# Chunk 0's joins: transposed blocks from VectorE, masks on GpSimd, loads and one MLP piece placed anew

## The chip, the cores and the metric

One core of a Trainium2 chip. The metric is the device time in microseconds (us) of one execution; lower is better. "PE" is TensorE (its weight loads are listed as "PEld"), "DVE" VectorE, "ACT" ScalarE, "POOL" GpSimd and "SP" SyncE, which issues most DMAs.

## The reference, cut to what matters

The input is `q`, `k`, `v` (4 batches, 8 heads, 768 tokens, 48 wide), `beta` (4, 8, 768), and two weights, 384x2048 and 2048x384. Everything is float32.

```
k_n = k / (norm(k) + 1e-6)
for t in range(768):                     # for each batch and head
    y[t]  = q[t] @ state
    v_old = k_n[t] @ state
    state = state + beta[t] * outer(k_n[t], v[t] - v_old)
x = y, heads side by side: 3072 tokens x 384
h = x @ w_in                             # 384 -> 2048
out = (h * sigmoid(h)) @ w_out           # 2048 -> 384
```

## The kernel before, in words

The 768 tokens are cut into 6 chunks of 128 tokens, each with two halves of 64 (`hf` is 0 or 1 in the code); the four batches form two groups of two (`g` is 0 or 1). Inside a chunk the recurrence becomes the solution of a triangular system for each batch and head. Its inverse `xi` is made once for a chunk out of blocks of 32 tokens; `inner` (L866) multiplies it with the values to give `z`, `update` (L886) brings the state forward, `old` (L932) and `new` (L945) give the outputs from the old state and from `z`. The outputs are turned into `xT`, the MLP's input with tokens along the free dimension. The MLP is cut into small pieces; one piece of its first half is three products `phid<-xT,w_in` (L1088), half of a bank, and after two pieces ACT applies silu (`gT`, L1098). Each float32 product is recorded as two matmuls and two weight loads.

**The joins of chunk 0.** Chunk 0 does not wait for a state, so its inverse is made by blocks in `joins(hf)` (L1539), a list of stages that are run one after the other. `corner` (L743) multiplies the off-diagonal 16-blocks and DVE adds the correction (L750). `turned` (L759) forms the transposed inverses of 32-blocks, as products, and copies them out of PSUM into `xes[0]` (in the trace `xe_y`), one copy by ACT and one by DVE for each group. `straight` (L772) forms the inverses themselves and copies four tiles for each group into `xi`, half by ACT (L554), half by DVE (L557). `merge_half` (L832) puts 32-blocks together to blocks of 64: the first product uses `xes[0]` and goes to `y`, the second uses `y` and goes to `xi`; each is again copied by one ACT and one DVE copy. PSUM banks come from three rooms: A (names `pl`, `py`, `px`), CC (`pb_c`) and M (`phid`, `pt`).

**After half 0's joins** come `inner` for half 0, then `first_outputs` (L910), whose products `py` become `xT` by an ACT copy (L554) and a DVE addition (L919). They need query blocks `ap`, which have been masked with `above` (L1524): four DVE multiplications of 128x512. Between stand turns of queries (`pt`, L510) that ACT copies to `stage` (L520).

**After that** a text of letters sets the order by hand, in `script`. The letters that matter: `j` is one step of `joins(1)`, `r` one MLP piece (three products), `s` a step of the solution for chunk 0, `f` a step of a narrowing, `b` its beginning, `l` a step of chunk 1's key lengths, `p` a step of its scores (L539), `q` a turn of its queries.

**Weights.** A weight arrives as 768 KB DMAs issued by SP (L292, L304). It is then narrowed: two ACT activations (L233, L234), then DVE operations (L238, L242) and a GpSimd integer addition (L246). A piece `w_in` number i must be narrowed before its MLP piece runs. ACT's two are placed by `begin_next`/`b`, the DVE ones by `fill`/`f`. The loads are in a list: each has a number, and is issued on SP once so many PE instructions have begun (`begun[0]`, 4 for a product, 2 for a turn). SP takes them in order, with the query loads (L144) among them. `pin` keeps each engine's instructions in the order in which the code writes them.

**Scattering.** For half 1 the odd heads' outputs go over `part` (L554), and SP's five DMAs (L925) into `xT`.

Of the kernel before, what the change touches and what calls it, by code (L numbers as in the profile page):

```python
# [19 lines left out]
def kernel(  # L20
# [10 lines left out]
    nc = tc.nc  # L31
# [660 lines left out]
    def invert_first(step):  # L692
# [62 lines left out]
        def turned(g, hf):  # L755

            pls = [bank(room, "pl") for room in (A, CC)]
            for i, n, k in heads(g, hf):
                pin(nc.tensor.matmul(  # L759
                    pls[k][rows[2 * k], T * i : T * (i + 1)], lhsT=up[rows[2 * k], n, :],  # L760
                    rhs=y[rows[2 * k], n, :], start=True, stop=True,
                ))
                yield
            for k, by in enumerate((by_act, by_dve)):
                by(of_half(xes[0][rows[2 * k]], g, hf, k), out_of(pls[k], rows[2 * k], T))

        def straight(g, hf):

            pls = [bank(room, "pl") for room in (A, CC)]
            for i, n, k in heads(g, hf):  # L770
                for j in (2 * k + 1, 2 * k):
                    pin(nc.tensor.matmul(  # L772
                        pls[k][rows[j], T * i : T * (i + 1)], lhsT=y[rows[j], n, :],
                        rhs=up[rows[j], n, :], start=True, stop=True,
                    ))
                    yield
            for odd in (1, 0):
                for k, by in enumerate((by_act, by_dve)):
                    j = 2 * k + odd
                    by(  # L780
# [4 lines left out]
        yield corner, turned, straight  # L785
# [33 lines left out]
    def merge_half(g, hf, second):  # L819
# [15 lines left out]
        for k, by in enumerate((by_act, by_dve)):  # L835
# [666 lines left out]
    for b in range(2, B):  # L1502
# [9 lines left out]
        (WINDOW + PACKET * 8 + -15, fetch_w_in, 6),  # L1512
        (WINDOW + PACKET * 9 + -45, fetch_w_in, 7),
        (WINDOW + PACKET * 10 + -15, fetch_w_out, 2),
        (WINDOW + PACKET * 15 + 45, fetch_w_out, 3),
        (WINDOW + PACKET * 15 + 60, fetch_w_out, 4),
# [5 lines left out]
    def masks(g, u):  # L1522
        to = aps[0, g][1][:, u]
        pin(nc.vector.tensor_tensor(  # L1524
# [3 lines left out]
    for n in range(Q):  # L1528
# [5 lines left out]
        if n == 14:  # L1534
            busy(1, done, Sync)
    corner, turned, straight = next(inv)
# [20 lines left out]
    def none():  # L1557
# [3 lines left out]
        lambda: (size_half(0, pins[seen_on]), begin_next(),),  # L1561
        lambda: (),
        lambda: (),
        lambda: (fill(1), fill(1),),
        lambda: (fill(1),),
        lambda: (),
        lambda: (fill(1),),
        lambda: (fill(1), begin_next(),),
        lambda: (),
        lambda: (),  # L1570
    ]))
    masks(0, 0)
    masks(0, 1)
    masks(1, 0)
    masks(1, 1)

# [150 lines left out]
    for text in (  # L1727
        "s f3 s q q s j32 b j20 r f j8 q f j4 f j16 r j44 b j4 q j4 r f r j22 f j12 f j8 f b j8 f j4 r j20 e r f j99 h f r f2 l s l r l p r l f p l s l2 f r3 l3 p l s l4 p l2 s r l f l4 f l f l2 p l s l2 s f r f r l r l2 p g i p l p f i p f l i r2 i r v f i3 r3 i r i r i3 b r2 f2 r2 i r2 i2 r2 i f b i r i3 f2 r2 f r3 f i2 r f i f r3 f r f i f i2 r i r i k i2 b z r2 i r i r z r i r2 b r t s r b r f s r2 t s m r m t2 r b m f t m s f b r m2 b m f s r m r s m4 s m3 c m4 s r t G m r2 m4 V m s r m r m t2",
# [68 lines left out]
```

## Time and profile before

| what | us |
|---|---|
| median of 3 runs | 631.42 (631.0 to 632.15) |
| the profiled execution's own time | 633.96 |
| its span (first to last instruction) | 631.8 |
| PE busy | 617.7 |
| DVE busy | 415.5 |
| ACT busy | 226.7 |
| POOL busy | 94.0 |

The granted clock of PE was 0.989 on average. Times in the profile count from the start of the span. A row of groups has: line, engine, operation, output and inputs with shapes and count; then busy us and mean ns; then the engine's idle time before them, with what ended it. A row of a timeline or chain begins with the start and the length in us. A row of the windows view has the stretch, its length, then busy us and count of PE, PEld, DVE, ACT and POOL (of PE and PEld alone where one line was asked for), the granted clock as a share of full speed, the share of the DMA engines' time that was busy, and GB/s. A row of the DMA queues has the queue, its kind, packets, MB and share of 16 engines. A row of DMA issues ends with KB each and the us from issue to landing.

### The profile page before, as it was taken

Reading aid. Unit: us, or ns where it says so; the run is one execution under the profiler, and the core shown is the slowest. Engines: PE = TensorE matmul, PEld = TensorE weight load, DVE = VectorE, ACT = ScalarE, POOL = GpSimd, SP = SyncE. Lnnn points to the kernel's source line nnn. Section 1 sums busy time; section 2 is a strip of 40 time slices with the busy share of each in tenths; the row PEclk is TensorE's granted clock in tenths of the full one; section 3 lists DMA queues with packets and bytes.
Section 4 is the critical chain, followed back from the end, with each engine's and each line's share of the span. In section 5 each row is a group of like instructions: output and inputs, shape, how many; then the busy total and the mean of one; then the engine's idle time right before and its main releaser. Section 6 shows DMA issues by size and latency. Waiting matters only on the chain.

```text
span 631.8 us, 21374 instructions
## 1 busy us (share of the span) xinstructions
PE 617.7 (98%) x9390; PEld 543.3 (86%) x9390; DVE 415.5 (66%) x927; ACT 226.7 (36%) x516; POOL 94.0 (15%) x101
## 2 busy tenths in 40 slices
PE   8889989999999999999999999999999999999997
PEld 5578778666799989989989989989989989988997
DVE  6886779999667974546975554976444983345432
ACT  4657873332441122451122451122452122454210
POOL 5234631335020020020020010020002000000000
PEclk9869999999999999999999999999999999999999
DMA  9656506350459360459141359433254024010011
GB/s 175 134 141 199 170 16 149 116 86 4 101 100 186 62 108 4 95 107 188 34 92 20 72 125 156 65 75 44 52 113 95 2 75 62 17 38 1 0 26 26
DMA packets 136941, 52.61 MB, mean 83 GB/s; under 512 B 108672, under 2 KB 130432, under 8 KB 136848
## 3 DMA queue, kind: packets, MB, share of 16 engines
q1 hardware_dynamic: 136512, 51.09, 39.6%
q8 instruction: 74, 1.21, 0.9%
q10 hardware_dynamic: 336, 0.15, 0.1%
q14 instruction: 19, 0.16, 0.1%
HBM read 39.09 MB, written 9.96 MB: 78 GB/s over the span
## 4 chain that ended last, share of the span: by engine, by line
PE 93%; SPq 2%; DMA 1%; issue 1%; ACT 1%; DVE 0%
PE phid L1088 34%; PE px L1200 17%; PE py L1200 13%; PE po L1132 5%; PE pb_c L866 3%; PE pa L539 2%; SPq L144 2%; PE pb_c L1303 2%; PE pb_c L854 2%; PE pyc L945 2%; PE pc L1303 2%; PE pb_c L1132 2%; PE pb_c L886 2%; PE pa L1303 1%; PE pyc L932 1%; PE px L808 1%
## 5 line engine op out<-in xcount | busy, mean ns | idle before, releaser
L1088 PE MATMUL phid<-xT,w_in 128*128 128x256 f32 x960 | 214.9, 382 | 1.9 <-issue 1.7
L1088 PEld LDWEIGHTS phid<-xT,w_in 128*128 128x128 f32 x960 | 180.2, 190 | 26.9 <-issue 2.8
L1098 ACT ACTIVATE gT<-phid 128x512 f32<-128x512 f32 x72 | 42.9, 597 | 115.2 <-PE phid L1088 106.2
L656 DVE SCALAR_TENSOR_TENSOR rank<-g,step,x 128x31 f32<-128x31 f32 (+15 forms) x124 | 49.8, 402 | 23.3 <-DMA g<-blocks 19.8
L1200 PE MATMUL px<-sums_of_w,sums_of_g 128*128 128x192 f32 x320 | 56.6, 329 | 0.0
L1200 PE MATMUL py<-w_out,sums_of_g 128*128 128x192 f32 x320 | 56.2, 328 | 0.0
L1200 PEld LDWEIGHTS px<-sums_of_w,sums_of_g 128*128 128x128 f32 x320 | 52.2, 190 | 0.4
L1200 PEld LDWEIGHTS py<-w_out,sums_of_g 128*128 128x128 f32 x320 | 52.3, 190 | 0.3
L661 DVE TENSOR_TENSOR x<-x,rank 128x31 f32<-128x31 f32 (+15 forms) x124 | 42.5, 342 | 4.3
L477 POOL TENSOR_TENSOR vf<-vf,n_slot 128x768 f32<-128x768 f32 x10 | 14.8, 1492 | 175.4 <-DMA vf<-in_v_dram 129.9
L1183 DVE TENSOR_TENSOR sums_of_g<-gT 128x384 f32<-128x384 f32 (+1 forms) x48 | 24.6, 540 | 14.6 <-ACT gT L1098 14.5
L498 DVE STREAM_TRANSPOSE kq<-stage 128x512 f32<-128x512 f32 x28 | 28.4, 1121 | 6.8 <-DMA stage<-in_q_dram 3.5
L554 ACT COPY xT<-pyc 48x128 f32<-48x128 f32 (+2 forms) x120 | 31.1, 259 | 1.6
L1211 DVE TENSOR_TENSOR o<-o,kept 128x192 f32<-128x192 f32 (+1 forms) x29 | 11.5, 425 | 26.7 <-ACT kept L1208 26.7
L560 POOL COPY g<-x 64x256 f32<-64x256 f32 x4 | 5.0, 1244 | 150.8 <-DVE x L664 150.8
L891 DVE TENSOR_TENSOR state<-state,pb_c 128x384 f32<-128x384 f32 x22 | 11.2, 550 | 24.6 <-PE pb_c L886 24.6
L866 PEld LDWEIGHTS pb_c<-vf,xi 64*64 64x64 f32 x736 | 23.3, 138 | 3.2 <-issue 2.3
L866 PE MATMUL pb_c<-vf,xi 64*64 64x48 f32 x736 | 24.9, 223 | 0.1
L1132 PE MATMUL po<-w_out,gT 128*128 128x384 f32 x64 | 23.7, 491 | 0.0
L1200 PE MATMUL py<-w_out,gT 128*128 128x192 f32 x128 | 23.4, 331 | 0.0
L859 DVE TENSOR_TENSOR vf<-vf,pb_c 128x384 f32<-128x384 f32 x22 | 11.2, 550 | 18.3 <-PE pb_c L854 15.5
L1200 PE MATMUL px<-w_out,gT 128*128 128x192 f32 x128 | 22.4, 327 | 0.0
(293 smaller groups left out, 1094.5 us busy)
## 6 DMA issues: line engine op xcount, KB each, us to landing
vf<-in_v_dram SPq DMA_DIRECT2D x48, 96.0 KB, 2.8
out_dram<-o SPq DMA_DIRECT2D x42, 96.0 KB, 2.2
w_out<-in_moe_w_in_dram SPq DMA_DIRECT2D x4, 768.0 KB, 5.0
sums_of_w<-in_moe_w_out_dram SPq DMA_DIRECT2D x4, 768.0 KB, 4.6
kb<-in_k_dram SPq DMA_DIRECT2D x12, 192.0 KB, 4.5
kb<-in_k_dram SPq DMA_DIRECT2D x24, 96.0 KB, 4.0
raw<-in_moe_w_in_dram SPq DMA_DIRECT2D x3, 768.0 KB, 6.8
blocks<-ap SPq DMA_DIRECT2D x32, 64.0 KB, 1.9
```

What stands on the lines that cost most here:

```text
L477: pin(nc.gpsimd.tensor_tensor(out=vf, in0=vf, in1=of, op=ALU.mult))
L498: pin(nc.vector.transpose(out=kqs[c, b][:, :, j, :].rearrange("p a (i m) -> p a m i", i=T), in_=src.rearrange("p a (m d) -> p a m d", d=D) ...
L554: return pin(nc.scalar.copy(to, of))
L656: pin(nc.vector.scalar_tensor_tensor(out=tv, in0=g[:, 0:m, m : m + 1].to_broadcast([P, m, n]), scalar=step[:, m : m + 1], in1=x[:, m : m + ...
L661: yield pin(nc.vector.tensor_tensor(out=x[:, 0:m, m:T], in0=x[:, 0:m, m:T], in1=tv, op=ALU.add))
L866: yield pin(nc.tensor.matmul(pz[rows, n * D : (n + 1) * D], lhsT=xis[g][rows, u * H + 2 * p + e, :], rhs=vfs[c][rows, hf, g * HB + u, p, : ...
L1088: pin(nc.tensor.matmul(ph[:, j * GT : (j + 1) * GT], lhsT=w_in[:, a, (2 * f + j) * P : (2 * f + j + 1) * P], rhs=xTs[c, hf][:, a, :], star ...
L1098: pin(nc.scalar.activation(out=hidden_of(c, hf, f), in_=ph[:], func=ACTF.Silu, scale=-0.5 if in_blocks(c) else 0.5))
L1132: pin(nc.tensor.matmul(pos[i][:, 0:DM], lhsT=hidden_of(0, hf, f // 2)[:, at : at + C], rhs=w_outs[f // HFF][:, f % HFF, :], start=(f == 0) ...
L1183: pin(nc.vector.tensor_tensor(out=sums_of_g[:, k, fs], in0=of[0], in1=of[1], op=op))
L1200: pin(nc.tensor.matmul(to, lhsT=at, rhs=quarter(f, *b) if isinstance(b, tuple) else sums_of_w[b][:, f], start=start and f == 0, stop=f == ...
L1303: pin(nc.tensor.matmul(to[:, i * GT : (i + 1) * GT], lhsT=left(a, slice(f, f + 1))[:, 0], rhs=right(b), start=start and i == 0 and n == 0, ...
```

## The change

Four things change.

1. `turned` goes. `straight` keeps its products, and DVE transposes its result out of PSUM, 32x32 blocks, into `xes[0]` (L766 after the change, two for each group and half). The four copies per group into `xi` are all ACT's. In half 0 both copies of the first merges are DVE's and both of the second are ACT's; in half 1 they stay as they were.
2. The masks of the queries are made by GpSimd, and inside half 0's joins (behind `corner` 0 and the first merge) instead of behind them. A filler product in the solution's step 14 goes.
3. The loads' numbers change, and query loads move to stand between the `w_in` loads 2 and 3 and behind 3. Narrowing steps move inside and behind half 0's joins.
4. In the script half 1's joins and pieces are placed anew, and one MLP piece moves from before chunk 0's second-half `inner` and `old` to behind them.

```diff
-        def turned(g, hf):
-
-            pls = [bank(room, "pl") for room in (A, CC)]
-            for i, n, k in heads(g, hf):
-                pin(nc.tensor.matmul(
-                    pls[k][rows[2 * k], T * i : T * (i + 1)], lhsT=up[rows[2 * k], n, :],
-                    rhs=y[rows[2 * k], n, :], start=True, stop=True,
-                ))
-                yield
-            for k, by in enumerate((by_act, by_dve)):
-                by(of_half(xes[0][rows[2 * k]], g, hf, k), out_of(pls[k], rows[2 * k], T))
...
+            for k in range(2):
+                pin(nc.vector.transpose(
+                    out=of_half(xes[0][rows[2 * k]], g, hf, k), in_=out_of(pls[k], rows[2 * k], T)
+                ))
             for odd in (1, 0):
-                for k, by in enumerate((by_act, by_dve)):
+                for k in range(2):
                     j = 2 * k + odd
-                    by(
+                    by_act(
...
-        for k, by in enumerate((by_act, by_dve)):
+        for k, by in enumerate((by_act, by_act) if second and hf == 0 else (by_dve, by_dve) if hf == 0 else (by_act, by_dve)):
...
-        (WINDOW + PACKET * 2 + 15, fetch_w_in, 2),
-        (WINDOW + PACKET * 3 + 90, fetch_w_in, 3),
-        (WINDOW + PACKET * 4 + 15, load_q, 1, slice(HB * 0, HB * 0 + HB)),
-        (WINDOW + PACKET * 5 + 0, load_q, 1, slice(HB * 1, HB * 1 + HB)),
-        (WINDOW + PACKET * 6 + -15, fetch_w_in, 4),
-        (WINDOW + PACKET * 7 + -15, fetch_w_in, 5),
...
+        (WINDOW + PACKET * 2 + 3, fetch_w_in, 2),
+        (WINDOW + PACKET * 2 + 251, load_q, 1, slice(HB * 0, HB * 0 + HB)),
+        (WINDOW + PACKET * 3 + 227, fetch_w_in, 3),
+        (WINDOW + PACKET * 4 + 211, load_q, 1, slice(HB * 1, HB * 1 + HB)),
+        (WINDOW + PACKET * 5 + 175, fetch_w_in, 4),
+        (WINDOW + PACKET * 6 + 87, fetch_w_in, 5),
...
-        pin(nc.vector.tensor_tensor(
+        pin(nc.gpsimd.tensor_tensor(
             out=to, in0=to, in1=above[:].unsqueeze(1).to_broadcast([P, H, W]), op=ALU.mult
...
-        if n == 14:
-            busy(1, done, Sync)
...
-            corner(0, hf), corner(1, hf), turned(0, hf), turned(1, hf), straight(0, hf), merge_half(0, hf, False),
-            straight(1, hf), merge_half(1, hf, False), merge_half(0, hf, True), merge_half(1, hf, True),
+            corner(0, hf), corner(1, hf), straight(0, hf), straight(1, hf),
+            merge_half(0, hf, False), merge_half(1, hf, False), merge_half(0, hf, True), merge_half(1, hf, True),
...
-        lambda: (size_half(0, pins[seen_on]), begin_next(),),
+        lambda: (size_half(0, pins[seen_on]), begin_next(), masks(0, 0), masks(0, 1)),
...
+        lambda: (masks(1, 0), masks(1, 1), fill(1), ),
```

The beginning of the script, up to the moved piece, before and after:

```
before  s f3 s q q s j32 b j20 r f j8 q f j4 f j16 r j44 b j4 q j4 r f r j22 f j12 f j8 f b j8 f j4 r j20
        e r f j99 h f r f2 l s l r l p r l f p l s l2 f r3 l3 p l s l4 p l2 s r l f l4 ...
after   s f s b f2 q q s j32 b j20 r f j8 q f j4 f r j32 b q j32 r f j16 r f f j16 f j16 f r j16 b
        e r f j99 h f r f2 l s l r l p r l f p l s l2 f r2 l3 p l s l4 p l2 s r2 l f l4 ...
```

**PE in half 0's joins.** Before, behind the corner products: the beginning of `turned` (L759), of `straight` (L772) and of the first merge (L832); the brackets name the engines that a row waits for.

```order
L743 MATMUL pb_c0_73<-sums_of_w_111,ap0_220 32x16 x2
L743 MATMUL pl_567<-sums_of_w_111,ap0_220 32x16 x2
L759 MATMUL pl_602<-sums_of_w_111 32x32 [waits DVE_49,Pool_49]
L759 MATMUL pb_c1_74<-sums_of_w_111 32x32 [waits DVE_49]
...
L759 MATMUL pl_622<-sums_of_w_111 32x32
L772 MATMUL pl_642<-sums_of_w_111 32x32 [waits PE_49]
...
L772 MATMUL pb_c0_73<-sums_of_w_111 32x32 x2
L832 MATMUL py_681<-xe_y_527,ap0_168 32x32 [waits Activation_49]
L832 MATMUL pb_c1_74<-xe_y_527,ap0_168 32x32 [waits DVE_49]
```

After, the same place; `straight` is L760 and the merge L824.

```order
L743 MATMUL pl_568<-sums_of_w_111,ap0_220 32x16 x2
L760 MATMUL pl_603<-sums_of_w_111 32x32 [waits DVE_49,Pool_49]
L760 MATMUL pl_603<-sums_of_w_111 32x32
L760 MATMUL pb_c0_73<-sums_of_w_111 32x32 [waits DVE_49]
...
L760 MATMUL pb_c1_74<-sums_of_w_111 32x32 [waits DVE_49]
...
L760 MATMUL pl_643<-sums_of_w_111 32x32 x2
L824 MATMUL py_682<-xe_y_526,ap0_168 32x32 [waits DVE_49]
L824 MATMUL pb_c2_75<-xe_y_526,ap0_168 32x32 [waits DVE_49]
```

`straight` follows the corners at once, for both groups, and the merge waits for DVE alone.

**ACT ahead of the first MLP piece.** Before, from the first `xT` copy on: two copies of turned queries, the second `xT` copy, then a narrowing.

```order
L554 COPY xT_874<-py0_845 128x3x128 [waits PE_49]
L520 ACTIVATE stage_80<-pt_877 128x512 [waits PE_49,Activation_49]
L520 ACTIVATE stage_80<-pt_883 128x512 [waits PE_49]
L554 COPY xT_874<-py0_889 128x3x128 [waits PE_49]
L233 ACTIVATE w_in_108<-w_out0_109 128x3x256 [waits DMAHW3_49]
```

After, from the same copy on, up to half 1's copies out of `straight`; the first L233 narrows weight 2, that behind `gT` weight 4.

```order
L554 COPY xT_833<-py0_807 128x3x128 [waits PE_49]
L233 ACTIVATE w_in_108<-w_out0_109 128x3x256 [waits DMAHW2_49]
L234 ACTIVATE w_out0_109<-w_out0_109,plus23_118 128x768
L520 ACTIVATE stage_80<-pt_839 128x512 [waits PE_49,Activation_49]
L520 ACTIVATE stage_80<-pt_848 128x512 [waits PE_49]
L554 COPY xT_833<-py0_854 128x3x128 [waits PE_49]
...
L1090 ACTIVATE gT_970<-phid_941 128x512 [waits DMAHW4_49,PE_49]
L233 ACTIVATE w_in_108<-w_out1_110 128x3x256 [waits DMAHW2_49]
...
L554 COPY xi_134<-pl_974 32x8x32 [waits DVE_49]
L554 COPY xi_134<-pb_c0_73 32x8x32 [waits DVE_49]
```

A narrowing now stands between the first `xT` copy and the two stage copies, and eight copies into `xi` stand together behind weight 4's narrowing.

**PE around the moved piece.** Before: behind L854 (the old state against the keys), and ahead of L886.

```order
L854 MATMUL pb_c0_73<-state1_91,kq_138 64x48
L1088 MATMUL phid_1317<-xT_874,w_in_108 128x256 x3
L1088 MATMUL phid_1395<-xT_874,w_in_108 128x256 [waits PE_49,Pool_49]
L1088 MATMUL phid_1395<-xT_874,w_in_108 128x256 x5
...
L932 MATMUL pyc_1490<-kq_138,state1_91 64x64
L1088 MATMUL phid_1523<-xT_874,w_in_108 128x256 [waits PE_49,Pool_49]
L1088 MATMUL phid_1523<-xT_874,w_in_108 128x256 x2
L886 MATMUL pb_c1_74<-z_78,kb0_76 48x48 [waits Activation_49]
```

After, the same two places (L846 was L854, L1080 was L1088, L878 was L886).

```order
L846 MATMUL pb_c1_74<-state1_91,kq_138 64x48
L1080 MATMUL phid_1248<-xT_833,w_in_108 128x256 x3
L1080 MATMUL phid_1326<-xT_833,w_in_108 128x256 [waits PE_49,Pool_49]
L1080 MATMUL phid_1326<-xT_833,w_in_108 128x256 x2
...
L924 MATMUL pyc_1417<-kq_138,state1_91 64x64
L1080 MATMUL phid_1326<-xT_833,w_in_108 128x256 x3
L1080 MATMUL phid_1454<-xT_833,w_in_108 128x256 [waits PE_49,Pool_49]
L1080 MATMUL phid_1454<-xT_833,w_in_108 128x256 x2
L878 MATMUL pb_c2_75<-z_78,kb0_76 48x48 [waits Activation_49]
```

Three products of L1088 have moved from the first place to the second.

More of the change, by code (lines that the diff above doesn't have):

```diff
@@ L783, in straight @@
                     )
-        yield corner, turned, straight
+        yield corner, straight
     slab = sum_room[:, AT_X : AT_X + SLAB]
@@ L1533 @@
             turn(1, n // 2 - 3, 0, M)
-        if n == 14:
-            busy(1, done, Sync)
-    corner, turned, straight = next(inv)
+    corner, straight = next(inv)
     pin(nc.gpsimd.memset(slab, 0.0))
@@ L1560 @@
     together(joins(0, [
-        lambda: (size_half(0, pins[seen_on]), begin_next(),),
+        lambda: (size_half(0, pins[seen_on]), begin_next(), masks(0, 0), masks(0, 1)),
         lambda: (),
         lambda: (),
-        lambda: (fill(1), fill(1),),
-        lambda: (fill(1),),
         lambda: (),
[L1567 to L1570, printed above, removed]
-    ]))
[L1572 to L1575, printed above, removed]
+        lambda: (masks(1, 0), masks(1, 1), fill(1), ),
+        lambda: (fill(1), fill(1), ),
+        lambda: (fill(1), ),
+        lambda: (fill(1), ),
+    ]))
     pieces = chained(hidden(0, 0), hidden(0, 1), project())
```

12 lines of the change are left out of this document (6 added, 6 removed).

## The prediction

> **What bounds the kernel now.** First the page's head: span, then the engines' shares.
>
> ```profile
> span 631.8 us, 21374 instructions
> PE 617.7 (98%) x9390; PEld 543.3 (86%) x9390; DVE 415.5 (66%) x927; ACT 226.7 (36%) x516; POOL 94.0 (15%) x101
> ```
>
> PE is busy for 98%, so time can only be won where it is idle, slow, or does work that can go. The change touches chunk 0; the stages of the windows view (us from the start; stage length, then busy us and count of PE, PEld, DVE, ACT, POOL; granted clock, DMA share, GB/s) show where that is.
>
> ```profile
> 31.16:41.23 10.07, 7.64 (x449) 7.11 (x449) 7.57 (x16) 6.16 (x13) 4.55 (x3) 0.73 0.53 160
> 41.23:49.31 8.08, 7.93 (x275) 7.55 (x273) 6.67 (x12) 4.09 (x9) 1.91 (x1) 0.71 0.53 104
> 49.31:65.95 16.64, 16.64 (x398) 13.27 (x402) 11.58 (x22) 11.55 (x23) 6.48 (x4) 1.00 0.72 213
> 65.95:83.58 17.63, 17.18 (x548) 14.44 (x548) 14.48 (x33) 15.08 (x27) 13.07 (x12) 1.00 0.37 118
> 83.58:91.89 8.31, 6.60 (x148) 5.69 (x149) 4.76 (x14) 7.17 (x18) 2.08 (x2) 1.00 0.11 27
> 91.89:631.80 539.91, 535.65 (x7246) 477.68 (x7240) 346.88 (x766) 165.00 (x391) 53.61 (x47) 1.00 0.37 73
> ```
>
> They are: half 0's joins; inner, first outputs and turns up to the first MLP piece; half 1's joins among seven pieces; the old state's part up to `new` (L945); the wait for the scattered tokens; the rest. The rest is dense (535.65 of 539.91), so what is gained by 91.89 stays gained to the end, if no later input is late. What idles PE before that stands in the chain of waits (start, length, what), whose "issue" pieces have no releaser:
>
> ```profile
> 34.80 1.13 issue
> 38.35 1.14 issue
> 48.61 0.57 DVE xT L919
> 49.31 1.53 PE phid L1088 x6
> 83.58 1.71 issue
> ```
>
> **What "issue" is.** The DMA view counts PE's instruction packets on q8. The rows are the whole span, then 33.1 to 60.9, 33.1 to 33.3 and 82.6 to 82.7 (narrow stretches put packets at 33.20, 37.20, 60.70, 82.65). Behind them stand two stretches of the windows view, between the first two stalls and just ahead of the third.
>
> ```profile
> q8 instruction: 74, 1.21, 0.9%
> q8 instruction: 8, 0.13, 2.2%
> q8 instruction: 1, 0.02, 37.9%
> q8 instruction: 1, 0.02, 74.6%
> 35.93:38.35 2.42, 2.42 (x127) 2.29 (x128) 2.33 (x5) 0.96 (x3) 0.98 (x1) 0.50 0.53 190
> 81.77:83.58 1.81, 1.81 (x128) 1.67 (x128) 1.78 (x4) 1.64 (x2) 1.73 (x2) 1.00 0.04 9
> ```
>
> 74 packets for 18,780 PE instructions (9390 matmuls and 9390 weight loads) are 254 each, and from one stall to the next PE runs 127 and 128: a packet is a block of 256. Eight come between 33.20 and 60.70, (60.70 − 33.20)/7 = 3.93 us each, while PE ran 255 in 2.42 us at half clock and 256 in 1.81 at full. The stalls end at 35.93, 39.49 and 85.29, which is 2.3 to 2.7 us behind a packet. **PE runs out of instructions there**: small products use up a block faster than one comes. So the count of instructions is itself a resource, and its place against the block borders matters.
>
> The Trainium skill, "Runtime: NRT & Kernel Launch", Instruction fetch mechanics, has 16 KiB blocks of 256 instructions and calls the fetch "mostly hidden". By that the three stalls, 1.13, 1.14 and 1.71, would not be there, and saved or moved instructions would win nothing at the third border: 629.8 in place of the 629.2 below. The trace differs, and decides.
>
> **Half 0's joins.** Removed are turned's 32 products a half, each two matmuls and two loads in the records (L759's rows, 31.16 to 49.31 and 49.31 to 65.95):
>
> ```profile
> 31.16:49.31 18.15, 1.60 (x64) 1.29 (x64) 0.72 0.53 135
> 49.31:65.95 16.64, 1.37 (x64) 1.18 (x64) 1.00 0.72 213
> ```
>
> That is 64 matmuls and 64 loads a half, 256 instructions in all, plus 4 of the filler: one block. Put in their place are four DVE transposes of 32x256 a half, on the path between straight's products and the merges.
>
> ```profile
> 33.06 0.36 DVE L750 SCALAR_TENSOR_TENSOR sums_of_w<-pb_c,second,pick 64x128 f32<-64x128 f32 x1
> L557 DVE COPY xe_y<-pb_c 32x256 f32<-32x256 f32 x8 | 3.4, 424 | 4.3 <-PE py L832 2.3 <-PE pb_c L759 1.6 <-PE pl L759 0.3
> L720 DVE STREAM_TRANSPOSE sums_of_w<-sums_of_w 128x1024 f32<-128x1024 f32 x1 | 1.9, 1949 | 0.0
> L716 DVE STREAM_TRANSPOSE sums_of_w<-sums_of_w 128x512 f32<-128x512 f32 x1 | 1.1, 1058 | 0.0
> L554 ACT COPY xi<-pl 32x256 f32<-32x256 f32 x8 | 2.9, 362 | 0.8 <-PE pl L772 0.5 <-PE pb_c L772 0.2
> ```
>
> No transpose out of PSUM and none of 256 columns is shown. The two transposes give 0.89 us per 512 columns and 0.17 fixed, so 256 columns 0.61. The plain copy from PSUM, 0.42, is the lower bound; 1.06, twice as many columns, the upper. I take 0.61.
>
> Corner ends on DVE at 33.06 + 0.36 = 33.42. Four transposes end at 33.42 + 4 × 0.61 = 35.86. The first merge cannot run before 35.93 anyway: it is at the block border that ended the first stall (its border moves by only three products against before). So the transposes just fit beneath the same stall. ACT's eight copies (8 × 0.36 = 2.9, each pair behind a transpose of its bank) end near 37.3. DVE copies the first merges 36.55 to 38.3, the second merges are made 37.45 to 39.25, and ACT's copies of them, 4 × 0.36, let inner begin at about 39.4, at the next border, 39.49. Before it began at 41.23. **Gain 1.8.** With transposes of 0.42 nothing more comes (the border holds), with 1.06 they end 1.8 later and the gain is near 0.3.
>
> The masks leave DVE for GpSimd.
>
> ```profile
> L1524 DVE TENSOR_TENSOR ap<-ap,above 128x512 f32<-128x512 f32 x4 | 2.5, 688 | 0.0
> 32.73 1.48 POOL L467 TENSOR_TENSOR vf<-vf,n_slot 128x768 f32<-128x768 f32 x1 [0.32 <-DVE sums_of_w L750]
> ```
>
> On GpSimd 512 columns by 1.48 for 768 are 1.0 each, four are 4 us in 34.2 to 38.4; bounds 0.69 (DVE's) and 1.48. Needed at first outputs, about 42, so hidden; even 4 × 1.48 is. What DVE loses is 2.5 us that held up only the copies of z.
>
> **From inner to the first piece: 0.5 given back.** The clock, from windows of 1 us:
>
> ```profile
> 36.00:37.00 1.00, 1.00 (x62) 1.00 (x66) 0.97 (x2) 0.14 (x1) 0.00 (x0) 0.50 0.93 360
> 46.00:47.00 1.00, 1.00 (x14) 0.87 (x9) 1.00 (x3) 0.73 (x3) 0.42 (x1) 1.00 0.63 126
> ```
>
> It is 0.50 from 35.9, behind the first stall, to 46.0, though PE is busy all of 36 to 37; these are three steps of 3.4 us. I let it open one step earlier, at 42.7, since the joins' last merges and inner now leave no stall in the step before. Then the first `py` is whole at 43.55. ACT's order there is new: `xT` copy, the narrowing of w_in 2, two stage copies, second `xT`.
>
> ```profile
> 46.84 1.08 ACT L520 ACTIVATE stage<-pt 128x512 f32<-128x512 f32 x2 [0.18 <-PE pt L510]
> 48.10 0.48 ACT L554 COPY xT<-py 128x384 f32<-128x384 f32 x1 [0.18 <-PE py L910]
> 48.47 0.90 ACT L233 ACTIVATE w_in<-w_out 128x768 f32<-128x768 f32 x1
> 49.27 1.00 ACT L234 ACTIVATE w_out<-w_out,plus 128x768 int32<-128x768 uint32 x1
> ```
>
> 43.55 + 0.48 + 1.8 (the pair overlaps by 0.1) + 1.08 + 0.48 + DVE's 0.57 = 47.96, so the piece starts near 48.0 against 49.31: **gain 1.3**. The narrowing on the path takes 1.8 and is what gives 0.5 of the 1.8 back. If the clock stays half until 46.0, the outputs come later, the piece starts near 48.65, gain 0.65.
>
> A rule speaks against the change: the Trainium skill, "TensorE: Matmul & The Clock Gate", Part 1, halves the clock after an idle window of about 3.4 us, free-running, and releases it after a busy one. The trace agrees that it falls behind a stall, but it stayed at half through a microsecond whose PE row reads fully busy. With less filler and fewer products the gate may reopen no earlier than before: by that 629.9, by my earlier step 629.2.
>
> **Half 1.** PE loses the 1.37 of turned. But all eight xi copies are ACT's now, and in the new order ACT has behind the second piece: gT 0.54 (the shape of a stage copy, 1.08/2), narrowing 1.8, stage 0.54, 8 × 0.36 = 2.9, gT 0.54, a `y` copy 0.36, in all 6.7 us. Laid out from the piece at 48.0 this runs from 51.95 to 58.65, and PE's second merges wait about 1.0 for it. Of 1.37 some 0.35 is left: the stage ends at 64.3 against 65.95, **gain 1.65**, and, with the same work behind it, L945 at 81.9 against 83.58.
>
> **The moved piece.** It is 6 matmuls, taken from ahead of the second half's inner and old state and put behind them, into the two blocks that end at the third stall. A piece lasts 1.53 us in the chain's row at 49.31 (its pitch is 1.49). The last of these blocks is used up in 1.81 us and its follower comes 1.71 late; with 1.49 more of work ahead of that border, 0.22 is left. Yet the tokens' odd heads must travel:
>
> ```profile
> 83.65 0.58 ACT L554 COPY part<-pyc 48x512 f32<-48x512 f32 x1 [0.23 <-PE pyc L945]
> 86.48 3.35 SPq L925 DMA_DIRECT2D xT<-part  x5
> xT<-part SPq DMA_DIRECT2D x33, 48.0 KB, 2.1
> ```
>
> The last of the five issues starts at 86.48 + 4 × 0.67 = 89.16 and lands 2.1 later, at 91.3: 7.7 after L945, hidden before. Now 81.9 + 7.7 = 89.6, with a semaphore 89.7, against 91.89: **gain 2.2**. PE itself, with 6.60 of work in that stage, would be there at 81.9 + 0.22 + 6.60 = 88.7, so 1.0 of waiting is new, and eats most of what the stall gives.
>
> **Loads.** SP's queue is reordered: w_in 2, q, w_in 3, q, then w_in 4 and 5 close together. ACT now takes w_in 4 ahead of the eight copies.
>
> ```profile
> 48.41 4.11 SPq L292 DMA_DIRECT2D w_out<-in_moe_w_in_dram  x2
> w_out<-in_moe_w_in_dram SPq DMA_DIRECT2D x4, 768.0 KB, 5.0
> raw<-in_moe_w_in_dram SPq DMA_DIRECT2D x3, 768.0 KB, 6.8
> ```
>
> I have it issued at 45.5 to 46.0 and landed at 51 (5.0) or 52.8 (6.8); ACT wants it at 52.55. No cost at 5.0, 0.25 at 6.8.
>
> **Sum.** 2.2 carried through the dense rest: the profiled execution took 633.96 (span 631.8 and 2.16 around it), so 631.76. It lay 2.54 above the runs' median of 631.42; on the median 631.42 − 2.2 = **629.2**.
>
> **Rivals.**
> - **More.** If the transposes are as cheap as a copy, the clock opens with the shorter stall and the tokens travel faster, the gain reaches one block, 3.93: 627.5. Against: two borders hold the early part whatever DVE does.
> - **Little.** Transposes of 1.06 leave 0.3 of the 1.8, and the narrowing takes that; half 1 gives 0.35, the moved piece 0.5: gain 0.85, 630.6. With the clock at half until 46.0 as well, 0.2 is left, 631.2. For: a clock of 0.50 through busy rows; no PSUM transpose in the trace.
> - **Slower.** ACT's narrowing of w_in 4 stands ahead of eight copies, a gT and the y copies. If the load lands behind 52.55, everything behind it slips by the same, and with it the second merges and all pieces. At 54.75 the 2.2 are gone; a load of 9 us issued at 46 decides it, and one landing at 57 gives 633.7. For: w_in 4 and 5 share the wires; the raw loads took 6.8. Against: 5.0 for the like ones.
> - **Not what it says.** Turned's products go, but PE is held by blocks, or by ACT, at every point where they stood: the joins end at the old borders, half 1 waits for ACT by all of the 1.37, and the tokens arrive as before: 631.4. Against: the border at 39.49 comes ahead of the old start of inner, 41.23.
>
> **How the numbers follow.** The forecast, gain 1.3 to 3.0, 630.1 to 628.4: 0.60. More: 0.06. Little, or not what it says, with loss below 0.2%: 0.18. Slower: 0.16. About 0.2%, 1.26 us, can be told from no change, so faster ends at 630.16. The range, 627.5 to 632.6, holds the first three cases but for some 0.04 at the upper gain; outside lie these and the 0.16 slower.
>
> **What would show it.** L766 transposes at 0.6 in the rows; the gap ahead of the first merge still ending near 35.9; inner at 39.5; the clock's row full by 43; the first piece at 48.0; no wait of ACT on w_in 4; the 1.71 stall gone and a wait of the first hf-1 piece on xT's DMA; 91.89 become 89.7. Wrong it is if transposes take 1 us, if ACT waits at w_in 4, or if q8's rows show the borders elsewhere.

## The result and the profile after

The changed kernel takes 633.43 us (median of 16 runs, 632.52 to 637.49) against 632.06 (16 runs, 630.67 to 634.02): ratio **1.0029**, 95% interval 1.0015 to 1.0043. It is slower by 0.3%, where 2.2 us faster was forecast.

First the head of its page and the stages cut as before: half 0's joins, inner to the first piece, half 1, up to the end of `new` (now L937), the wait for tokens, the rest.

```profile
span 631.7 us, 21115 instructions
PE 614.4 (97%) x9260; PEld 540.3 (86%) x9260; DVE 413.0 (65%) x919; ACT 227.9 (36%) x520; POOL 98.8 (16%) x105
```

```profile
29.72:39.02 9.30, 6.08 (x307) 5.40 (x296) 6.64 (x14) 4.46 (x11) 7.73 (x6) 0.69 0.57 131
39.02:49.50 10.48, 9.42 (x277) 8.64 (x273) 6.51 (x11) 6.13 (x12) 3.74 (x2) 0.62 0.44 115
49.50:65.97 16.47, 15.91 (x335) 12.36 (x338) 12.83 (x19) 13.44 (x25) 7.82 (x5) 1.00 0.76 242
65.97:83.47 17.50, 17.12 (x549) 14.43 (x549) 14.35 (x36) 13.82 (x26) 11.87 (x12) 1.00 0.28 94
83.47:92.69 9.22, 7.71 (x153) 6.36 (x153) 6.19 (x19) 7.07 (x18) 1.84 (x1) 1.00 0.10 26
92.69:631.70 539.01, 534.46 (x7236) 476.55 (x7236) 343.81 (x757) 165.07 (x391) 53.71 (x47) 1.00 0.38 73
```

PE is busy for 3.3 us less, yet the span is the same: the work went and waiting came. The joins end at 39.02 in place of 41.23, as hoped. The second stage gives it back: 10.48 us in place of 8.08 (10.41 if it is counted to the piece's first matmul). The third is 0.17 shorter by these cuts, 0.10 from first matmul to first matmul, the fourth 0.13 shorter, and the fifth 0.91 longer. Its chain of waits, and one row that sums PE's waits:

```profile
27.77 1.06 DVE sums_of_w L716
33.27 2.02 issue
39.47 0.91 issue
49.50 1.49 PE phid L1080 x6
89.08 3.48 DMA xT<-part
92.69 2.40 PE phid L1080 x10
```

```profile
PE phid L1080 <- DMA xT<-part: 1.5, 1, 1.5
```

The first stall has grown from 1.13 to 2.02, the second one now stands inside `inner`, and the third (1.71) has become a wait of 1.5 for the tokens' DMA. The new operations cost this:

```profile
L766 DVE STREAM_TRANSPOSE xe_y<-pb_c 32x256 f32<-32x256 f32 x4 | 1.8, 448 | 0.1
L766 DVE STREAM_TRANSPOSE xe_y<-pl 32x256 f32<-32x256 f32 x4 | 1.7, 437 | 1.6 <-PE pl L760 1.5
L1516 POOL TENSOR_TENSOR ap<-ap,above 128x512 f32<-128x512 f32 x4 | 4.9, 1260 | 0.0
```

**Comparing executions.** The profiled execution of before (633.96) lies near the upper end of the 16 runs above. A second one, of another session (e5 below, 633.92), lies near the middle of that session's runs (630.95 to 636.49, median 633.56). In both the clock is at half for one window early (18.7 to 22.1, 19.6 to 23.0), and the corner ends 5.4 us behind L716 instead of 4.2; the changed kernel's profile has no such window, and neither has that of e6 below, which is before with two loads exchanged. So times below are counted from the start of the solution's transpose (L716), and e6 stands beside before.

### The profile page after: what moved, and what is told of

Same layout as the page of the kernel before. It is cut to its first block, busy times and chain, and to the rows that moved or that the text cites. A ratio compares the mean times of both kernels' runs of the same rounds, so it can differ in the third digit from the quotient of the medians.

```text
span 631.7 us, 21115 instructions
## 1 busy us (share of the span) xinstructions
PE 614.4 (97%) x9260; PEld 540.3 (86%) x9260; DVE 413.0 (65%) x919; ACT 227.9 (36%) x520; POOL 98.8 (16%) x105
## 4 chain that ended last, share of the span: by engine, by line
PE 91%; DVE 3%; ACT 2%; DMA 1%; issue 1%; SPq 1%; POOL 0%; POOLq 0%; DVEq 0%
PE phid L1080 32%; PE px L1192 17%; PE py L1192 13%; PE po L1124 5%; PE pb_c L858 3%; PE pa L539 2%; PE pb_c L846 2%; PE pb_c L1295 2%; PE pyc L937 2%; PE pc L1295 2%; PE pb_c L1124 2%; PE pb_c L878 2%; PE pa L1295 1%; PE pyc L924 1%; PE px L800 1%
## 5 line engine op out<-in xcount | busy, mean ns | idle before, releaser
L1080 PE MATMUL phid<-xT,w_in 128*128 128x256 f32 x960 | 215.2, 382 | 1.5 <-DMA xT<-part 1.5
L1080 PEld LDWEIGHTS phid<-xT,w_in 128*128 128x128 f32 x960 | 180.0, 190 | 26.9 <-issue 2.7
```

What stands on the lines that cost most here:

```text
L1080: pin(nc.tensor.matmul(ph[:, j * GT : (j + 1) * GT], lhsT=w_in[:, a, (2 * f + j) * P : (2 * f + j + 1) * P], rhs=xTs[c, hf][:, a, :], star ...
```

## The experiments

**e5: before, unchanged, profiled a second time.**

> The kernel before, unchanged, profiled a second time, to see how much of a stage's time differs from one execution to the next. Theory (fetch): its blocks of PE instructions follow each other by 3.6 to 4.0 us as before, inner starts within 0.5 us of 41.2. Rival (the first profile of before was an unlucky one): its clock is half for two windows or fewer in 33 to 49, and the first piece starts 1 us or more ahead of 49.31, so that the kernel with the query load later won nothing on it.

Inner starts 13.17 us behind L716 (13.22 in the first), the first piece at 21.65 (21.30): the second stage repeats at 8.1 to 8.5 us. Its blocks step by 3.56 again. The rival is not borne out here. In e6, without the early window, the first piece does come 1.7 us ahead of 49.31, though with three half windows in 33 to 49 and with two loads exchanged.

**e1: the query load behind w_in 3's.**

```diff
         (WINDOW + PACKET * 2 + 3, fetch_w_in, 2),
-        (WINDOW + PACKET * 2 + 251, load_q, 1, slice(HB * 0, HB * 0 + HB)),
-        (WINDOW + PACKET * 3 + 227, fetch_w_in, 3),
+        (WINDOW + PACKET * 3 + 60, fetch_w_in, 3),
+        (WINDOW + PACKET * 3 + 227, load_q, 1, slice(HB * 0, HB * 0 + HB)),
```

> The changed kernel with the first query load (three DMAs) moved behind w_in 3's load, the order of before. Theory (fetch): the early query load lies on the instruction fetch. In the changed kernel the block that ends the stall at 35.29 is followed 5.09 us later by the next one (40.38), where before took 3.56 (35.93 to 39.49). With the query load later that step falls to 3.6 to 4.2, inner's stall of 0.91 goes to under 0.2, and the kernel is 0.5 to 1.0 us faster than the changed one (ratio to before about 1.002). Rival (gate): the time is lost to the half clock from 33.3 to 46.9, whatever the fetch does; then the stall moves, the piece at 49.5 stays within 0.3, and the time stays at 1.003.

Ratio 1.0000 (0.9979 to 1.0021): the 0.29% is gone, more than the theory had forecast. The two intervals overlap, so the time alone doesn't settle it; the stage does: the first piece starts 20.27 us behind L716, in the changed kernel 21.66. The chain of waits has no stall left in `inner`:

```profile
33.11 1.43 issue
47.95 1.49 PE phid L1080 x6
87.54 2.75 DMA xT<-part
```

The step from the block's arrival (34.54) to the next border (crossed at 38.44 without a wait) is 3.90 us, in the changed kernel 5.09 (35.29 to 40.38). The DMA view shows what lies in it; the first row is the changed kernel from 35.29 to the instruction packet at 37.42, the second e1 from 34.54 to 38.28, where `inner` starts.

```profile
DMA packets 2061, 0.46 MB, mean 215 GB/s; under 512 B 2032, under 2 KB 2032, under 8 KB 2059
```

```profile
DMA packets 305, 0.61 MB, mean 164 GB/s; under 512 B 16, under 2 KB 16, under 8 KB 303
```

2032 packets under 512 B, nearly all of them rows of the query load, lie between the border and the instruction packet, which comes 2.13 us behind the border; in e1 it comes 1.18 behind (35.72).

**e6: before with the same two loads exchanged.**

```diff
-        (WINDOW + PACKET * 3 + 90, fetch_w_in, 3),
-        (WINDOW + PACKET * 4 + 15, load_q, 1, slice(HB * 0, HB * 0 + HB)),
+        (WINDOW + PACKET * 3 + 3, load_q, 1, slice(HB * 0, HB * 0 + HB)),
+        (WINDOW + PACKET * 4 + 15, fetch_w_in, 3),
```

> The kernel before with only the order of two loads changed: the first query load at the first merge (count 1216), w_in 3's load behind it where the query load stood (1484). Theory (fetch): the query load's short rows lengthen the fetch of the next block from 3.6 to about 5 us, a stall grows by 1 to 1.5 us, ratio 1.0015 to 1.003. Rival (the order of loads is not what costs; the clock or ACT is): 0.999 to 1.0005, stalls as before.

Ratio 1.0000 (0.9980 to 1.0020): the theory as I had put it fails. Its step is 3.59 us, with the small packets in it. The row from its block's arrival, 34.45, to the instruction packet at 35.56 shows a difference that can explain it:

```profile
DMA packets 205, 0.39 MB, mean 354 GB/s; under 512 B 13, under 2 KB 13, under 8 KB 205
```

Here the load was issued at 34.79, behind the border, and 1635 small packets came behind the instruction packet, not ahead of it. In the changed kernel its number (1208) lies five instructions ahead of the border (1213), and it was issued at 33.28, in the stall. So it is the order of the two, and not the early load as such, that goes with the stall; e6 is the only kernel with the load just behind the border. Over all profiles: in the six with the early query load and this border (the changed kernel, e2, e3, e4, f2, g1) the packet comes 1.84 to 2.42 us behind the border and the step is 4.54 to 5.35 us, each with a stall in `inner`; in eight with the later load (e1, f1, f3, f4, g2, g3, g4, h1) the packet comes 1.15 to 1.60 us behind and the step is 3.7 to 4.0, with no stall there. The Trainium skill, "Runtime: NRT & Kernel Launch", Instruction fetch mechanics, gives the sequencer a DMA queue of its own and calls the fetch "mostly hidden"; here it has its own queue (q8), but its packet comes later with those small packets ahead of it, and it is not hidden.

**e2: the filler product put back.**

```diff
             turn(1, n // 2 - 3, 0, M)
+        if n == 14:
+            busy(1, done, Sync)
```

> The changed kernel with the one filler product at step 14 put back. Theory (gate): without the filler PE is busy for 0.23 us of 30 to 31 and runs dry at 33.27, so the clock falls one window earlier (33.3 in place of 35.9) and stays at half for four windows in place of three; with the filler it falls at 35.9 or later and is half for three, the first piece starts about 1.5 us earlier than 49.5 and the ratio to before is 0.998 to 1.001. Rival (fetch): the filler only delays the corner by 1.2 us, the block border still comes at about 35.3 to 36, the first piece stays at 49.5 and the ratio at 1.003.

1.0025 (1.0005 to 1.0045), inner's stall is 0.61 in place of 0.91. The clock still falls at 33.3, and though it stays at half for three windows only, the first piece comes 0.4 us sooner behind L716 and not 1.5. The gate theory falls here, and more clearly by comparing e3 with the changed kernel: rows of 1 us, first the changed kernel, which is at half from 33.3 to 46.9, four windows; then e3, from 33.6 to 43.9, three.

```profile
46.00:47.00 1.00, 1.00 (x9) 0.67 (x7) 0.73 (x2) 1.00 (x2) 1.00 (x1) 0.53 0.16 35
```

```profile
44.00:45.00 1.00, 1.00 (x31) 0.93 (x22) 0.97 (x2) 0.86 (x3) 0.00 (x0) 1.00 0.00 0
```

In both the first piece comes 21.7 us behind L716 (21.66, 21.68). A window of half clock more or less moved nothing, since in e3 PE then waited, 1.19 us for ACT's `xT` copy and 0.54 for a block.

**e3: the MLP piece back.**

```diff
-... l2 f r2 l3 p l s l4 p l2 s r2 l f ...
+... l2 f r3 l3 p l s l4 p l2 s r l f ...
```

> The changed kernel with the moved MLP piece back where it was. Theory (tokens): the piece only trades the stall of 1.7 us behind L937 for a wait of 1.5 us on the tokens' DMA, so the first piece of half 1's tokens starts within 0.4 us of 92.7 and the time is the same within 0.5 us. Rival (the move gains what the stall cost): 1.0 to 1.5 us slower than the changed kernel, ratio to before about 1.005.

1.0020 (0.9998 to 1.0042), which can't be told from the changed kernel's 1.0029. The stall is back, and the first piece of half 1's tokens comes at 91.81, not within 0.4 us of 92.7:

```profile
83.25 1.74 issue
91.81 3.22 PE phid L1080 x14
```

From the end of L937 (here and in before all but its last product, which stands behind the stall) to that piece are 8.56 us here, 9.22 in the changed kernel, 8.44 in e1, 8.38 in before. The move traded a stall for a wait.

The wait is longer than the stall because the last of the tokens' five DMAs lands 3.48 us behind its issue at 89.08, in e3 1.99 (89.27 to 91.26). One of PE's instruction packets lies in that stretch, 89.08 to 92.56, at 90.32:

```profile
q8 instruction: 1, 0.02, 2.2%
```

In e3 the packet comes at 92.02, behind the landing. It is so in all 20 profiles: in twelve such a packet comes 1.1 to 1.9 us behind the last issue, and the landing takes 2.57 to 3.98 us; in the eight others none comes until the landing is done or, in e7, all but done, and it takes 1.98 or 1.99. So the moved piece moved the packet onto the tokens' DMA; that the packet is the cause is not tested by itself.

**e4: the narrowing behind the second xT copy**, and **f1: that and the query load later.**

```diff
-        "s f s b f2 q q s j32 b j20 ...
+        "s f s q q s b f2 j32 b j20 ...
```

> The changed kernel with the narrowing of w_in 2 begun behind the second xT copy, as before, and no longer ahead of the two stage copies. Theory (ACT order): the pair takes 1.7 us on the path to the second xT, so the first piece starts 0.5 to 1.5 us earlier than 49.5, ratio to before 1.001. Rival (gate or fetch): the second first-outputs products end at 47.9 by PE alone at half clock, ACT has slack there, and the first piece and the time stay (1.003).

> The changed kernel with both the query load behind w_in 3's and the narrowing of w_in 2 behind the second xT copy. Theory (blocks): with the narrowing alone moved, PE waited 1.75 us at the corner products ahead of the first piece for the block that starts at instruction 1981; with the query load alone moved that block came at 47.65. It was asked for when PE crossed 1725, at 44.8 us, which neither edit alters, so the first piece starts within 0.4 us of 47.95 (20.3 us behind the solution's first transpose) and the ratio is 1.000. Rival (ACT's order is the rest of the loss): the piece starts 1.0 us or more earlier than 47.95 and the ratio is 0.998.

e4: 1.0022 (1.0000 to 1.0045), the first piece unmoved. f1: 1.0002 (0.9987 to 1.0017), the first piece at 47.80, 20.1 behind L716, where e1 has 20.3: as the block theory said. But f1 has an early half window, and its corner ends 0.6 us later than e1's, so some 0.8 us of gain may hide there. e4's chain of waits:

```profile
47.40 1.75 issue
49.46 1.49 PE phid L1080 x6
```

What ACT gives is taken by the next border, 1981, a few corner products ahead of the first piece.

**f2: the first piece ahead of that border** (with the narrowing later), **f3: with the query load later too, f4: with half 1's copies shared as well.**

```diff
-        "s f s b f2 q q s j32 b j20 r f j8 ...
+        "s f s q q s j24 r b f2 j8 b j20 f j8 ...
```

> The changed kernel with the narrowing of w_in 2 moved and, besides, the first MLP piece placed ahead of the last eight corner products, that is ahead of the block border at 1981. Theory (blocks): the piece (12 instructions, 1.5 us) then runs while the block is awaited, starts at 47.3 to 47.8 in place of 49.46, the stall of 1.75 falls under 0.5, and the kernel is 1.2 to 1.8 us faster than with the narrowing alone moved (1.0022): ratio 0.9995 to 1.000. Rival (the stall is not a wait for instructions but for xT or a bank): the piece starts at 49 to 49.5 all the same and the ratio stays at 1.002.

> Both: query load behind w_in 3's, narrowing moved, first piece ahead of the border. Theory (blocks): first merge at 34.5, inner without a stall at 38.3, first piece at 46.2 to 46.8, ratio 0.997 to 0.998, faster than both kernels. Rival: the next border or ACT in half 1's joins takes it back, the end of L937 lies within 0.4 us of that with the query load alone moved, and the ratio is 1.000.

> The same, and in half 1's joins the copies into xi shared by ACT and DVE as before. Theory (ACT in half 1): in the changed kernel ACT runs without a gap from 53.5 to 60.3, and the second merge waits 0.6 us for its y copy; with four of the eight copies on DVE that wait goes and the end of half 1's joins comes 0.5 to 1.0 us sooner, ratio 0.0010 under the kernel without it. Rival (PE and the pieces are the bound there): no difference beyond 0.0005, and DVE's transposes and narrowing come later by the 1.7 us that the copies take.

f2's piece starts at 47.30, 19.7 behind L716 and 2 us sooner than e4's: PE did wait for instructions there. But f2 is slower, 1.0054 (1.0026 to 1.0082). PE then waits at the following border, ACT waits 2.1 us for weights, and the clock is at half from 57.0 to 60.4; the runs don't separate the three. The border:

```profile
47.30 1.53 PE phid L1080 x6
53.60 1.82 issue
```

f3 is no better: 1.0051 (1.0028 to 1.0075), and its piece comes at 48.55, not at 46.2 to 46.8. With the piece moved up, w_in 4's load got its number behind it, was issued at 50.27, and ACT waited for it with the eight copies queued behind:

```profile
55.32 0.93 ACT L233 ACTIVATE w_in<-w_out 128x768 f32<-128x768 f32 x1 [1.57 <-DMA w_out<-in_moe_w_in_dram]
```

That is the wait of the prediction's rival on the slower side, made by my own edit, but not its price: f4 measured 0.9993 (0.9979 to 1.0006), with ACT waiting 1.9 us there. From f3 to f4 the clock's later half windows (61.1 to 71.3 in f3) go too, so what f3 lost stays open, and the gain isn't the copies' alone.

**g1: half 1's copies shared, alone; g2: with the query load later; g3: f4 with w_in 4's load some 115 instructions earlier.**

```diff
-                    by_act(
+                    (by_act if hf == 0 or k == 0 else by_dve)(
```

> The changed kernel with half 1's eight copies into xi shared by ACT and DVE again, nothing else. Theory (ACT in half 1): ACT's copies, 56.31 to 59.33 in the changed kernel, shrink by 1.5 us, the second merge no longer waits 0.6 us, the end of half 1's joins comes 0.5 to 1.5 us earlier, ratio 1.0005 to 1.002 where the changed kernel has 1.0029. Rival (blocks and clock ahead of the first piece are all of the loss): within 0.0005 of 1.0029.

> Query load behind w_in 3's and the copies shared. Theory (both are costs of their own, in different stages): first piece 20.3 us behind the solution's first transpose as with the query load alone, the stage of half 1 shorter by 0.5 to 1.5 us, ratio 0.998 to 0.999, faster than both kernels. Rival (the stages hide each other): 1.000 as with the query load alone.

> Query load later, copies shared, narrowing later, first piece ahead of the border, and w_in 4's load issued some 115 instructions earlier, since with the piece ahead its number came behind the piece and ACT waited 1.6 to 1.9 us for it. Theory (load of w_in 4 is next in line): ACT's wait at its narrowing falls under 0.3 us, the end of half 1's joins comes 1.5 us sooner than in the run without (0.9993), ratio 0.997 to 0.998. Rival (the load lies behind the queries in SP's queue, whatever its number): it is issued at most 0.5 us sooner, and the ratio stays at 0.999.

g1: 1.0006 (0.9981 to 1.0032); g2: 0.9982 (0.9961 to 1.0004); g3: 0.9996 (0.9975 to 1.0017). The times settle little. The stage from the first piece to the first L878 does: 16.62 us in g1 and 16.35 in g2, against 16.47 in the changed kernel and 16.57 in before. ACT's full queue isn't on the path there; PE's pieces are. g3 has the earliest piece (19.6 behind L716), and ACT's wait for w_in 4 is gone as its theory said, but its time is no better than f4's. g2 is the best ratio, not clear of 1.

**e7 and e8: three loads into the idle stretch at 27 to 33 us**, in the changed kernel and in before (e7's edit; e8's is the like).

```diff
-        (WINDOW + PACKET * 2 + 3, fetch_w_in, 2),
-        (WINDOW + PACKET * 2 + 251, load_q, 1, slice(HB * 0, HB * 0 + HB)),
-        (WINDOW + PACKET * 3 + 227, fetch_w_in, 3),
+        (WINDOW + PACKET * 0 + 207, load_q, 1, slice(HB * 0, HB * 0 + HB)),
+        (WINDOW + PACKET * 1 + 3, fetch_w_in, 2),
+        (WINDOW + PACKET * 2 + 3, fetch_w_in, 3),
```

> The changed kernel with the first query load, w_in 2 and w_in 3 each issued one place earlier: the query load at about 27 us and w_in 2 at about 29.5, where the profiles show the DMA engines idle, w_in 3 at 31.6. Theory (fetch): the blocks between 33 and 45 come by 3.6 to 4.0 us each, inner starts by 39.3, the first piece by 48.2, ratio 0.996 to 0.999, a kernel faster than both. Rival (gate): the first piece stays at 49 to 49.5 and the ratio at 1.002; a third case is that traffic at 27 to 33 only moves the late block to an earlier border, first merge at 36 or later.

> The kernel before with the same three loads moved into the idle stretch (query load at 27 us, w_in 2 at 30, w_in 3 at 33). Theory (fetch): the block of the stall at 38.35 comes sooner, as no weight load lies beside it, ratio 0.997 to 0.999. Rival (joins end by DVE and ACT, not by blocks): the same as before within 0.001.

e7: 1.0002 (0.9983 to 1.0021); e8: 1.0024 (1.0006 to 1.0043). The third case of e7 came true in both: the first block became the late one, stalls of 2.58 and 2.87 us in place of 2.02 and 1.13. Both executions also have early half windows, one in e7 and two in e8, so how much of that is the traffic's isn't shown. Moving the loads into the idle stretch won nothing.

**g4: the joins and the masks alone**, with load order, filler, piece, narrowing of w_in 2 and shared copies in half 1 as before; the later loads' numbers and the script's placing of half 1's joins stay as in the changed kernel.

> Of the change only the joins (transposes for products, fills among them) and the masks on GpSimd stay; the query load, the filler, the MLP piece, the narrowing and half 1's shared copies are as before. Theory (the transposes gain, the placements lose): ratio 0.997 to 0.999. Rival (blocks take back what the products gave, whatever the placements): 1.000 within 0.001.

0.9997 (0.9975 to 1.0020): the rival's number. Inner starts 11.00 us behind L716 (e6: 12.10), the first piece 20.63 (e6: 19.91); PE waits 1.0 at the border at 1981.

**h1: e1 with the masks on DVE behind the joins; h2: before with the masks on GpSimd** (h2's edit; h1's is the reverse, and the four calls stand behind the joins).

```diff
-        pin(nc.vector.tensor_tensor(
+        pin(nc.gpsimd.tensor_tensor(
             out=to, in0=to, in1=above[:].unsqueeze(1).to_broadcast([P, H, W]), op=ALU.mult
```

> The changed kernel with the query load behind w_in 3's and the four masks on DVE again, behind the joins. In all kernels with the masks on GpSimd the end of the span came 3.95 us or more behind the last matmul's end, in the kernel before and its relatives 3.52; the difference lies in GpSimd's last instructions. Theory (four more GpSimd instructions shift its program so that its last ones are waited for): 3.52 again with the masks on DVE, 0.4 us off the time (0.0007), and nothing lost in the joins, as DVE then holds up only z. Rival (the end depends on something else of the change, the order of loads or PE's count): 3.95 still.

> The kernel before with only the four masks moved to GpSimd, where they stand. Theory: the end comes 3.95 us behind the last matmul in place of 3.52, and the masks, about 4.9 us on GpSimd, now end at 46 or later, behind the need of the first outputs at 43 to 44, so that the first piece comes 2 us later and the ratio is 1.003 to 1.004. Rival (the end does not follow the masks): 3.52.

h1: 1.0049 (1.0028 to 1.0071); h2: 0.9991 (0.9974 to 1.0008). First DVE in h1, then GpSimd in h2:

```profile
40.09 3.87 DVE L1516 TENSOR_TENSOR ap<-ap,above 128x512 f32<-128x512 f32 x4
```

```profile
38.04 5.16 POOL L1524 TENSOR_TENSOR ap<-ap,above 128x512 f32<-128x512 f32 x4
```

In h1 the masks hold back the copies of `z` to 43.99, and everything behind. On GpSimd they are worth 0.5% in the changed kernel (h1 against e1), and cost nothing in before: there they end at 43.2, just in time, so my 1.003 was wrong. The end of the span lies 3.53 us behind the last matmul in h1, 3.83 in h2, 3.51 to 3.53 in before, e5, e6 and e8, and 3.95 to 3.98 in the changed kernel and most of its relatives (4.7 to 4.9 in f4, g2, g3). So 0.3 to 0.4 us follows the masks' engine, and in those three something else adds 0.8 to 0.9; why is open in both.

## Why the prediction was wrong, point by point

- **Block of 256 instructions as the bound: right** for the stalls ahead of the first piece and the one behind L937; the tokens' wait is a DMA's.
- **Transposes: 0.61 taken, 0.44 measured**, the price of the copy and the lower bound. **Masks: 1.0 taken, 1.23 to 1.26 measured**, hidden as said (33.57 to 38.49).
- **Inner at 39.4: right (39.02), but in part by luck, and not the gain.** The border that was to let it begin lies behind its start. The 1.8 was counted from an execution with an early window of half clock. Behind L716 inner starts 1.97 sooner than in that execution, and 0.85 sooner than in e6 (12.10 to 11.25).
- **The step that failed: "From inner to the first piece: 0.5 given back".** Inner to piece was to take 8.6 us and took 10.41 (11.25 to 21.66; before 8.08). I took the borders' times from the trace of before as if they were fixed, so that inner could start at "the next border, 39.49". But they move with what PE has run before, and with what lies on the DMA queues. With half a block fewer instructions ahead of it this border lies inside `inner`, behind its first few products (39.02 to 39.47), and with the query load issued ahead of the border before, its block came at 40.38, 5.09 us behind the last one, not 3.56. Undoing that alone takes the ratio to 1.000 (e1). None of the four rivals had this load ahead of an instruction packet.
- **Where the other 2.2 us went.** With the load out of the way the stage still takes 9.0 to 9.6 us (f1, e1, g4), in e6 7.81. In e1 the 1.80 more are, nearly in full, 0.76 of waiting for ACT's `xT` copy, 0.34 of waiting at border 1981, which the kernel before crossed without a wait, and 0.66 in the first outputs and the turn between them, which now run while the clock is at half (41.68 to 45.47, 3.79 us; in e6 43.19 to 46.32, 3.13; both clocks open at 43.9). At border 1981 PE waits 0.3 to 1.0 us in f1, e1, g2 and g4. In before that border came 12.0 to 12.7 us behind the arrival of 1213's block (e6, before, e5); in these four 12.2 to 13.2. So what is run sooner is waited for again; the rival "Not what it says" was right there, at 631.4, and I gave it too little.
- **The narrowing on ACT's path: hidden in the changed kernel.** It was to take 1.8 from the path; moved away, the piece didn't move (21.66 and 21.67 in e4).
- **The clock at 42.7: wrong (46.9), and without effect** (e3 beside the changed kernel). The half stretches are 13.65 and 10.24 us, four and three times 3.41, as the Trainium skill, "TensorE: Matmul & The Clock Gate", Part 1, has its window; that the change lengthens them, as I had its rule speak, the runs don't show: before has three in this stretch and the changed kernel four, but e2, e3 and e4, like it up to where the clock falls but for the filler in e2, have three.
- **Half 1: 0.35 forecast, 0.10 measured** (16.57 to 16.47).
- **The moved piece: 0.5 forecast, no gain measured** (e3). The stall went as said, but the last of the five DMAs took 3.48 us to land (2.75 in e1), not the 2.1 of the median, with an instruction packet beside it, so the tokens came 9.22 behind L937 in place of 7.8.
- **Nothing was forecast for the end**: 0.44 us there.
- **w_in 4: no wait of ACT in the changed kernel.** The wait of the rival on the slower side came only with a piece moved up (f2, f3, f4), and its price isn't shown (f4 against g3).

Added up against e6, from L716 on: inner −0.85, the second stage +2.60, half 1 −0.10, the fourth stage −0.13, tokens +1.19, the rest −0.16, the end +0.43, together 2.98, which is 603.93 − 600.95; e6's profiled execution was the fastest of its runs, so the medians lie closer. What remains open: why the step from packet to block differs (2.2 to 3.0 us), and what of the last 0.2% is run-to-run, as the intervals of e1 to g4 are about that wide. g1, which keeps the early query load, measured 1.0006 (0.9981 to 1.0032).

## What to carry to other kernels

Where short instructions make PE starve for code, count them, mark the borders of 256, and treat the fetch as one more DMA with a queue: a load of many small rows is issued behind the instruction packet, not between a border and it. A block's time isn't a constant of the trace: it moves with what runs before it, so half a block of work removed ahead of three borders can be waited for again at the third. A small DMA that PE waits for can meet an instruction packet in the same way. And take the base from an execution that lies at the median, or count stages from an event that the change can't touch.

## What the runs showed of the hardware that was not expected

- A DVE transpose of 32x256 from PSUM took 0.44 us, hardly more than DVE's copy of the same tile (0.42), although one of 128x512 in SBUF took 1.06.
- An instruction packet of 16 KB came 2.13 us behind the border with 2032 small packets ahead (1.84 to 2.42 in six kernels), 1.1 to 1.65 in the others.
- The last DMA of the tokens landed in 2.57 to 3.98 us in the twelve profiles with an instruction packet of PE 1.1 to 1.9 us behind its issue, in 1.98 or 1.99 in the eight others.
- Four more GpSimd instructions at 34 to 43 us went with 0.3 to 0.44 us more at the very end of the span.
- The first 26 us, alike in all kernels, ran with or without a window of half clock at 18 to 23, and with it the corner came 0.6 to 1.2 us later (4.2 behind L716 without, 4.8 to 4.9 in f1, g1 and e7, 5.4 in before); with two such windows, to 25, it came 5.8 (f4) and 6.4 (e8) behind.
